# Five weight loads into freed work space, a product on another engine, a new head and order, and identity transposes in a drain

## The chip, the cores and the metric

One core of one Trainium2 chip runs the whole program. The metric is the device time in microseconds (us) of one execution. TensorE (PE) multiplies and transposes, VectorE (DVE), ScalarE (ACT) and GpSimd (POOL) do the rest, SyncE (SP) issues the loads and stores. Inputs and outputs lie in HBM; engines work on SBUF, and PE writes PSUM.

## The reference

All values are float32. A pack attention with 8 batches, 8 heads, 576 tokens of 64 channels and 32 packed queries, and then a soft mixture of 8 experts on the 4608 tokens of 512 channels that come out:

```python
def sm_attn(qq, kk, vv):
    s = scale * qq @ kk.transpose(0, 1, 3, 2)
    a = np.exp(s - s.max(-1, keepdims=True))
    return (a / (a.sum(-1, keepdims=True) + 1e-9)) @ vv
p_packed = sm_attn(p, k, v)              # 32 rows for each head
x = sm_attn(q, p_packed, p_packed)       # as [4608, 512]
logits = x @ phi                         # [4608, 32]
slot_input = softmax(logits, axis=0).T @ x           # 32 slots, 4 for each expert
slot_out[e] = relu(slot_input[e] @ w1[e]) @ w2[e]    # w1 512x1024, w2 1024x512
out = softmax(logits, axis=1) @ slot_out
```

## The kernel before

The attention runs in 8 steps `i` (two batches `dd` = i // 2, four heads). A step transposes k on DVE (`kt`), multiplies it with the packed queries (`s1`, line 355), takes maximum and exponential (`mx1`, `e1`), transposes that (`ap`), multiplies with v (`m`, 408), divides (`rz`, `ppa`, `pp`), transposes (`pt`, `ptc`), transposes q (`qp`, `qc`), multiplies (`s2`, 526) and does the second softmax: maximum `mx2`, subtraction `sb`, exponential `e2`, sum `z2` (on POOL, in the last step on DVE), reciprocal `rc`, product `n2` (POOL); `a2p` and `a2c` transpose it. After every second step the logits of one `dd` are made (`lg`, 631) and joined to a running softmax over all tokens: `f1` and `f3` take the maximum on DVE, `f2` and `f4` turn it around on PE, `f5` takes the exponential `dL` and its sum `zg` on ACT, `rw` (line 701, DVE) multiplies the sum into a 128x32 matrix, `f6` (706) sums that over the partitions on PE, `fd` transposes `dL`, `gr` (734), `rt`, `gt` (753), `rb` and `gs` (780) add the slots' inputs, `fl` copies the logits.

The order of all these pieces on each engine is the text `ORDER`: one word for each piece, with its indices, its PSUM bank after @ and the copying engine after a colon. Each engine executes its share in that order and waits where an input isn't there. What comes last I call the drain: from the last `s2` to the line that writes `xz`, the input of the experts.

The loads go through one ring of 120 KB for each partition, in the order p, then k, q, v of each step, then the 16 halves of w1 (1 MB each) and w2 in 17 pieces (15 of 1 MB, two of 0.5 MB). `pump()` issues the next load on SP as soon as its place in the ring has been released in program order. 14 pieces of the weights fit while the attention still holds its work tiles in the pools `wpool` and `dpool`; the 19 others wait until `layer1a` has read the first ones. After the drain, `layer1a` (868) and `layer1b` make the hidden values, `layer2` (920) runs for experts 0 to 6, `cq` and `cp` prepare the softmax over the slots for the output (`cT`), four tiles at a time, and `last2` (997), line 1010 and line 1018 end the last expert. Then 36 products write the output (1042, 1049), and SP stores it (1044, 1055).

```python
def f_rw(dd, j, bank, eng):
    nc.vector.tensor_scalar_mul(rw, rep[:, 0], zg)
...
for n, e in enumerate(range(1, E - 1)):
    cq(4 * n + 8)
    layer2(e)
    cp(4 * n + 8, "av"[n % 2])
cq(32)
cp(32, "a")
```

Of the kernel before, what the change touches and what calls it, by code (L numbers as in the profile page):

```python
# [15 lines left out]

ORDER = """
p.0.0 p.1.0 px.0.0@7 p.2.0 p.3.0 px.1.0@6 pc.0.0:v kt.0.0  # L20
kt.0.1 px.2.0@7 pc.1.0:v kt.0.2 px.3.0@6 pc.2.0:v kt.0.3 pc.3.0:v
s1.0.0@0 qp.0.0@7 mx1.0.0 qp.0.1@6 qc.0.0:a qp.0.3@5 qc.0.1:a qp.0.4@7
e1.0.1 qc.0.3:v qp.0.2@6 qp.0.5@4 e1.0.0 qc.0.4:v qc.0.2:a ap.0.0@7
rz.0.0 qc.0.5:a ap.0.1@6 apc.0.0:a ap.0.2@5 apc.0.1:a m.0.0@6 apc.0.2:a
kt.1.1 m.0.1 kt.1.0 m.0.2 kt.1.2 ppa.0.1 ppa.0.0 pp.0.1
pp.0.0 kt.1.3 pt.0.0 ptc.0.1:a s1.1.0@0 ptc.0.0:a mp.0.0 mx1.1.0
mm.0.0:a s2.0.0@5 e1.1.1 s2.0.1 e1.1.0 qp.1.1@4 mx2.0.0 ap.1.0@3
qc.1.1:a ap.1.1@2 apc.1.0:a ap.1.2@4 sb.0.0 apc.1.1:a qp.1.0@3 apc.1.2:a
# [1060 lines left out]
```

## Time and profile before

| what | us |
|---|---|
| median of 3 runs (lowest, highest) | 238.25 (237.82, 238.55) |
| the profiled execution's own time | 237.79 |
| its span, first to last instruction | 236.0 |
| busy PE / DVE / ACT / POOL | 182.5 / 126.1 / 92.8 / 47.4 |

The busy times are shares of the whole span. The kernel has stages with different limits, so the rows further down are read by stage. A row of the timeline gives the start and the length of a group of instructions of one line, and in brackets how long the engine had been idle before it and for whom. [...]

### The profile page before, as it was taken

What the parts mean: (1) busy time and instruction counts of PE and PEld (TensorE: products, weight loads), DVE (VectorE), ACT (ScalarE), POOL (GpSimd) and SP (SyncE); (2) the same over time, 40 slices, a digit from 0 to 9 for tenths busy, and PEclk for the clock granted to TensorE, in tenths of its full rate; (3) what the DMA queues carried; (4) which work ended last, traced back from release to release, by engine and by line L of the source; (5) the groups of instructions that cost most, each with busy time, mean ns of one, the idle gap of its engine ahead of it and who ended that gap; (6) DMA issues with size and microseconds to landing.
All of it is one profiled execution on the core that took longest, in us unless ns stands there. A gap on an engine that the chain in (4) does not pass through costs nothing.

```text
span 236.0 us, 6352 instructions
## 1 busy us (share of the span) xinstructions
PE 182.5 (77%) x2715; PEld 117.0 (50%) x2715; DVE 126.1 (53%) x248; ACT 92.8 (39%) x228; POOL 47.4 (20%) x76
## 2 busy tenths in 40 slices
PE   0987989999799995999997577899959655989000
PEld 0665858777496773486866533423311111457000
DVE  1785769676872886464757942772133022159200
ACT  0073847657568574347673422011100000059300
POOL 8100071535305344005458200000000000000000
PEclk9999999999999997799999675579995996599755
DMA  7999999999999999922919000099999998019997
GB/s 161 383 392 391 390 391 390 390 387 391 391 392 388 405 406 403 406 90 60 417 62 350 13 0 0 3 330 431 422 418 422 422 422 332 6 59 409 416 416 301
DMA packets 24683, 72.29 MB, mean 306 GB/s; under 512 B 4176, under 2 KB 4432, under 8 KB 22736
## 3 DMA queue, kind: packets, MB, share of 16 engines
q1 hardware_dynamic: 24080, 71.83, 79.0%
q8 instruction: 21, 0.34, 0.6%
q10 hardware_dynamic: 576, 0.07, 0.2%
q14 instruction: 6, 0.05, 0.1%
HBM read 62.46 MB, written 9.44 MB: 305 GB/s over the span
## 4 chain that ended last, share of the span: by engine, by line
PE 46%; DMA 17%; DVE 17%; ACT 8%; issue 2%; POOL 1%; POOLq 1%; ACTq 0%; DVEq 0%; SPq 0%
DMA ring<-in_moe_w_dram 15%; PE ps L355 6%; PE ps L408 5%; PE ps L868 4%; PE ps L498 4%; PE ps L526 4%; PE ps L1049 3%; PE ps L734 3%; PE ps L607 3%; DVE rw L701 3%; PE ps L386 3%; DVE kT L341 2%; ACT a L369 2%; DMA ring<-in_p_dram 2%; DVE a L557 2%
## 5 line engine op out<-in xcount | busy, mean ns | idle before, releaser
L920 PE MATMUL ps<-ring,hT 128*32 128x512 f32 x112 | 17.7, 722 | 9.4 <-DMA ring<-in_moe_w_dram 9.4
L583 POOL TENSOR_TENSOR zt<-a 128x576 f32<-128x576 f32 x7 | 9.9, 1408 | 72.2 <-ACT a L575 72.2
L341 DVE STREAM_TRANSPOSE kT<-ring 128x576 f32<-128x576 f32 x32 | 23.2, 754 | 1.0 <-DMA ring<-in_k_dram 1.0
L498 PE MATMUL ps<-ident,ring 128*128 128x128 f32 x144 | 20.4, 279 | 0.0
L526 PE MATMUL ps<-ppT,qT 128*64 128x64 f32 x576 | 18.5, 223 | 0.3 <-ACT mm L291 0.3
L598 POOL TENSOR_TENSOR a<-a,zs 128x1152 f32<-128x1152 f32 (+1 forms) x8 | 16.2, 2020 | 12.3 <-DVE zs L594 10.6
L291 ACT COPY qT<-ps 128x512 f32<-128x512 f32 (+1 forms) x43 | 17.9, 477 | 1.7 <-PE ps L498 1.3
L408 PE MATMUL ps<-ring,a1T 64*64 64x128 f32 x576 | 18.2, 272 | 0.3 <-ACT a1T L291 0.3
L291 ACT CAST cT<-ps 128x512 fp32r<-128x512 f32 x6 | 3.5, 586 | 37.1 <-PE ps L946 37.1
L526 PEld LDWEIGHTS ps<-ppT,qT 128*64 128x64 f32 x576 | 17.5, 138 | 0.7 <-ACT mm L291 0.4
L408 PEld LDWEIGHTS ps<-ring,a1T 64*64 64x64 f32 x576 | 15.8, 133 | 2.7 <-DVE rz L421 0.8
L868 PE MATMUL ps<-ring,xz 128*32 128x512 f32 x128 | 16.7, 678 | 0.4 <-DVE xz L953 0.4
L498 PEld LDWEIGHTS ps<-ident,ring 128*128 128x128 f32 x144 | 15.7, 141 | 2.5 <-issue 1.3
L355 PE MATMUL ps<-kT,pT 32*32 32x288 f32 x512 | 16.4, 446 | 0.7 <-issue 0.4
L366 DVE TENSOR_REDUCE nm<-ps 128x2 f32<-128x1152 f32 x8 | 10.9, 1356 | 10.3 <-PE ps L355 8.7
L549 DVE TENSOR_REDUCE mx<-ps 128x36 f32<-128x1152 f32 (+1 forms) x9 | 12.8, 1421 | 4.5 <-PE ps L526 3.4
L369 ACT ACTIVATE a<-ps,nm 128x576 f32<-128x576 f32 x16 | 11.8, 743 | 6.7 <-DVE nm L366 6.7
L607 PE MATMUL ps<-ident,a 128*128 128x128 f32 x72 | 11.9, 303 | 2.8 <-POOL a L598 1.4
L295 DVE CAST cT<-ps 128x512 fp32r<-128x512 f32 x3 | 2.1, 692 | 21.3 <-PE ps L946 21.3
L291 ACT COPY a1T<-ps 128x384 f32<-128x384 f32 x24 | 10.1, 487 | 6.3 <-PE ps L386 6.3
L291 ACT COPY a2T<-ps 128x384 f32<-128x384 f32 x23 | 10.0, 484 | 4.0 <-PE ps L607 4.0
L586 POOL TENSOR_TENSOR zt<-zt 128x288 f32<-128x288 f32 (+2 forms) x21 | 11.2, 535 | 1.6
(130 smaller groups left out, 286.1 us busy)
## 6 DMA issues: line engine op xcount, KB each, us to landing
ring<-in_moe_w_dram SPq DMA_DIRECT2D x31, 1024.0 KB, 13.7
ring<-in_k_dram SPq DMA_DIRECT2D x16, 576.0 KB, 11.9
ring<-in_q_dram SPq DMA_DIRECT2D x16, 576.0 KB, 11.9
ring<-in_v_dram SPq DMA_DIRECT2D x16, 576.0 KB, 12.0
out_dram<-ring SPq DMA_DIRECT2D x10, 768.0 KB, 8.3
ring<-in_moe_w_dram SPq DMA_DIRECT2D x2, 512.0 KB, 18.0
out_dram<-ring SPq DMA_DIRECT2D x2, 512.0 KB, 3.8
ring<-in_p_dram SPq DMA_DIRECT2D x1, 512.0 KB, 4.3
```

The lines of the kernel that those rows point to most:

```text
L291: nc.scalar.copy(dst, src)
L341: nc.vector.transpose(kT[:, b2, :, c].rearrange("p m (t r) -> p m t r", t=T), view(f"k{i}.{b2}").rearrange("p (m t c d) -> p m t c d", m=2 ...
L355: nc.tensor.matmul(ps[32 * y : 32 * y + 32, z, 0 : 32 * T], pT[rs, dd, m, b2, g, c], kT[rs, b2, m, c], start=(c == 0), stop=(c == 1),)
L369: nc.scalar.activation(a1[:, :, x].rearrange("p t (h r) -> p h t r", h=2), s1v[:, x].rearrange("p h (t r) -> p h t r", t=T), AF.Exp, bias= ...
L408: nc.tensor.matmul(ps[64 * b2 : 64 * b2 + 64, b + x, 0:P].rearrange("p (m d) -> p m d", m=2), a1T[rs, t, b2], view(f"v{i}.{b2}").rearrange ...
L498: nc.tensor.transpose(ps[:, bank, o : o + P], view(f"q{i}.{b2}")[:, P * y : P * y + P], ident)
L526: nc.tensor.matmul(psf[64 * b2 : 64 * b2 + 64, o : o + 2 * NS].rearrange("p (u s) -> p u s", u=2), qT[:, b2, n, 64 * x : 64 * x + 64], col ...
L549: nc.vector.tensor_reduce(part(mxs[i % 2], c), s2v(i, c), axis=AX.X, op=ALU.max)
L598: (nc.vector if eng == "v" else nc.gpsimd).tensor_tensor(a, a, z.unsqueeze(3).broadcast_to([P, a.shape[1], a.shape[2], NS]), op=ALU.mult)
L607: nc.tensor.transpose(ps[:, bank, o : o + P], a2s[i // NG % 2][:, t, i % NG].rearrange("p c s -> p (c s)"), ident,)
L868: nc.tensor.matmul(ps[32 * a : 32 * a + 32, b + nh, :], xzf[:, (4 * e + a) * NSLOT : (4 * e + a + 1) * NSLOT], wv[:, j, nh * 512 : (nh + 1 ...
L920: nc.tensor.matmul(ps[32 * a : 32 * a + 32, SO, :], hTf[:, (NJ * e + j) * NSLOT : (NJ * e + j + 1) * NSLOT], w2v(e, j), start=(e == 0 and ...
```

## The change

Five parts. (1) At the point `late`, where `wpool` is given up, five tiles `ext` of 8 KB for each partition are laid into its space, and the next five pieces of the weights are loaded there. Two tiles that the drain still writes or reads change pools for it: `a2_0` and `ppT` go to `wpool`, so that their space is freed too, and the clearing of `hT` and the copy `identr` move behind the drain. `cT` lies in the space of `ext` afterwards, so all `cp` now come after `layer2(1)`, two for each expert. (2) `rw` is made on ACT, inside `f5`. (3) `p` is loaded in four pieces, three of them behind the first k; the first exponential, on a dummy, comes before ACT issues the loads of `phi`; `sel` is built earlier. (4) A new `ORDER`; `s2` is made, and its maximum and subtraction taken, in two halves that may lie in different banks; `gt` is split into two halves by columns. (5) `w.n` puts n transposes of the identity on PE, into a bank that nobody reads, 75 in all, from the last `gr` but one to the experts' first product.

```diff
@@ ORDER: two lines of the last third @@
-fd.3.0 rw.3.0 gr.3.0@4 f6.3.0 rt.3.1:a rt.3.0:a gz.3.0 gt.3.0
+w.6.0@6 f1.3.0 f2.3.0 w.14.0@6 f3.3.0 f4.3.0 w.12.0@6 f5.3.0
...
@@ loads @@
-    loads.append(("p", B * NG * D, p.rearrange("b (g h) s d -> (h s) (b g) d", g=NG)))
+    loads.append(("p0", 2 * NG * D, rows_p(0)))
     for i in range(NSTEP):
         for b2 in range(2):
             loads.append((f"k{i}.{b2}", 2 * T * D, rows9(k, i, b2)))
+        if i == 0:
+            for dd in range(1, ND):
+                loads.append((f"p{dd}", 2 * NG * D, rows_p(dd)))
...
@@ head @@
+    nc.vector.memset(ones, 1.0)
+    first = const.tile([P, 1], F32, name="first")
+    nc.scalar.activation(first, ones[:, 0:1], AF.Exp)
...
-    a2s = [dpool.tile([P, T, NG, 4, NS], F32, name=f"a2_{x}") for x in range(2)]
+    a2s = [wpool.tile([P, T, NG, 4, NS], F32, name="a2_0"), a2_1]
...
-    ppTs = [dpool.tile([P, 2, 2, 4, NS], F32, name=f"ppT_{x}") for x in range(2)]
+    ppTs = [wpool.tile([P, 2, 2, 4, NS], F32, name=f"ppT_{x}") for x in range(2)]
...
@@ f_f5 (and f_rw is gone) @@
+        nc.scalar.mul(rw, rep[:, 0], zg)
         if dd > 0:
             nc.scalar.activation(al, ps[:, b, W2 : W2 + NSLOT], AF.Exp)
-    def f_rw(dd, j, bank, eng):
-        nc.vector.tensor_scalar_mul(rw, rep[:, 0], zg)
...
@@ new @@
+    def f_w(n, j, bank, eng):
+        for _ in range(n):
+            nc.tensor.transpose(ps[:, bank, 0:P], ident, ident)
...
@@ f_late @@
-        hT = late.tile([P, E, NJ * NSLOT + SPE], F32, name="hT")
-        nc.gpsimd.memset(hT, 0.0)
...
+        ext = [extp.tile([P, 2 * FF], F32, name=f"ext_{x}") for x in range(NEXT)]
+        if "at" in state:
+            state["off"] = state.pop("at")[1]
+        for x in range(NEXT):
+            key, width, src = loads[state["next"]]
+            where[key] = (ext[x], width)
+            load(ext[x][:, 0:width], src)
+            state["next"] += 1
...
@@ experts @@
-    cp(0, "a")
-    cq(4)
     layer1b(0)
...
-    for n, e in enumerate(range(1, E - 1)):
-        cq(4 * n + 8)
+    layer2(1)
+    ees.close()
...
+    cp(0, "a")
+    for e in range(2, E - 1):
+        for n in range(2):
+            t0 = 8 * (e - 2) + 4 * n
+            if t0 + 4 < NT:
+                cq(t0 + 4)
         layer2(e)
-        cp(4 * n + 8, "av"[n % 2])
-    cq(32)
-    cp(32, "a")
+        for n in range(2):
+            t0 = 8 * (e - 2) + 4 * n
+            if t0 + 4 < NT:
+                cp(t0 + 4, "av"[n])
```

SP's queue from the last v load to the first store, before (`ring` is the load ring, `x16` a count of like loads):

```order
L167 DMA ring<-in_v_dram 128x2x576 x2
L167 DMA ring<-in_moe_w_dram 128x2x1024 x16
L167 DMA ring<-in_moe_w_dram 128x2048 x15
L167 DMA ring<-in_moe_w_dram 128x1024 x2
L1044 DMA out_dram<-ring 128x256 x2
```

And now:

```order
L158 DMA ring<-in_v_dram 128x2x576 x2
L158 DMA ring<-in_moe_w_dram 128x2x1024 x14
L158 DMA ext_1891<-in_moe_w_dram 128x2x1024
L158 DMA ext_1892<-in_moe_w_dram 128x2x1024
L158 DMA ext_1893<-in_moe_w_dram 128x2048
L158 DMA ext_1894<-in_moe_w_dram 128x2048
L158 DMA ext_1895<-in_moe_w_dram 128x2048
L158 DMA ring<-in_moe_w_dram 128x2048 x12
L158 DMA ring<-in_moe_w_dram 128x1024 x2
```

The two last halves of w1 and the three first pieces of w2 go to `ext`; 14 pieces (13 MB) are left for the ring behind them, where there were 19 (18 MB).

PE in the drain, before, from the last `lg` to the first product of the experts (643 is `f2`, 665 and 673 `f4`, 734 `gr`, 706 `f6`, 753 `gt`, 780 `gs`):

```order
L631 MATMUL ps<-a2T_144,mm_154 32x288 x4
L643 MATMUL ps<-ident,nml 1x128
L665 MATMUL ps<-ones,m_175 128x1
L673 MATMUL ps<-dm,ones 128x32
L734 MATMUL ps<-a_1_142,d 32x256 x18
L706 MATMUL ps<-rw,ones 128x32
L753 MATMUL ps<-rep,rt 128x32 x4
L780 MATMUL ps<-rb,pp_148 64x64 x2
L780 MATMUL ps<-rb,pp_149 64x64 x2
L868 MATMUL ps<-ring,xz 32x512 x48
```

And now, from behind the last `lg` to before `gs` (662 is `f2`, 684 and 692 `f4`, 723 `f6`, 751 `gr`, 771 `gt`, 782 the identity transposes):

```order
L782 MATMUL ps<-ident 128x128 x6
L662 MATMUL ps<-ident,nml 1x128
L782 MATMUL ps<-ident 128x128 x14
L684 MATMUL ps<-ones,m_185 128x1
L692 MATMUL ps<-dm,ones 128x32
L782 MATMUL ps<-ident 128x128 x12
L723 MATMUL ps<-rw,ones 128x32
L782 MATMUL ps<-ident 128x128 x2
L751 MATMUL ps<-a_1_108,d 32x256 x18
L782 MATMUL ps<-ident 128x128 x6
L771 MATMUL ps<-rep,rt 64x32 x8
L782 MATMUL ps<-ident 128x128 x6
```

Between any two products of the chain stands a group of transposes, `f6` comes ahead of `gr`, and `gt` has eight products of half the columns.

SP's head, before, with what each load waits for (DMAHW0 to 3 are the four `phi` loads, 4 to 7 the first loads of SP, and so on around):

```order
L167 DMA ring<-in_p_dram 128x16x64
L167 DMA ring<-in_k_dram 128x2x576 x2
L167 DMA ring<-in_q_dram 128x2x576
L167 DMA ring<-in_q_dram 128x2x576 [waits DMAHW0_49]
L167 DMA ring<-in_v_dram 128x2x576 [waits DMAHW1_49]
L167 DMA ring<-in_v_dram 128x2x576 [waits DMAHW2_49]
```

And now:

```order
L158 DMA ring<-in_p_dram 128x4x64
L158 DMA ring<-in_k_dram 128x2x576 x2
L158 DMA ring<-in_p_dram 128x4x64
L158 DMA ring<-in_p_dram 128x4x64 [waits DMAHW0_49]
L158 DMA ring<-in_p_dram 128x4x64 [waits DMAHW1_49]
L158 DMA ring<-in_q_dram 128x2x576 [waits DMAHW2_49]
L158 DMA ring<-in_q_dram 128x2x576 [waits DMAHW3_49]
```

Both loads of q now stand behind a wait for a `phi` load, where the first of them stood ahead of these waits.

## Rows read from the trace of the kernel before

**Rows 1.** The span by stretches; columns: stretch, length, busy times, PEclk, DMA share, GB/s.

```profile
23.30:87.00 63.70, 60.01 (x1273) 46.80 (x1272) 46.52 (x81) 40.46 (x102) 22.73 (x25) 1.00 1.05 392
87.00:99.00 12.00, 8.77 (x134) 5.18 (x132) 7.83 (x16) 4.87 (x17) 4.24 (x6) 0.72 1.02 407
99.00:125.80 26.80, 26.22 (x521) 21.32 (x523) 14.86 (x32) 17.74 (x47) 9.84 (x12) 1.00 0.47 174
125.80:150.80 25.00, 17.07 (x187) 11.67 (x183) 15.06 (x36) 5.97 (x16) 5.09 (x5) 0.69 0.17 67
150.80:174.50 23.70, 22.46 (x188) 7.38 (x188) 11.59 (x24) 4.00 (x6) 0.00 (x0) 0.89 0.89 355
174.50:196.70 22.20, 14.00 (x88) 3.29 (x88) 4.26 (x14) 1.17 (x2) 0.00 (x0) 0.85 1.01 421
196.70:210.30 13.60, 10.84 (x59) 4.92 (x60) 3.29 (x8) 2.07 (x5) 0.00 (x0) 0.62 0.21 84
210.30:236.00 25.70, 8.47 (x35) 5.88 (x34) 9.49 (x16) 9.89 (x20) 0.00 (x0) 0.70 0.91 367
```

**Rows 2.** The chain of waits in the experts' stage: start, length, what.

```profile
176.86 19.83 DMA ring<-in_moe_w_dram
```

**Rows 3.** The timeline of the head: start, length, engine, line, operation, count, idle before.

```profile
0.73 2.67 ACTq L234 DMA_DIRECT2D phi_sb<-in_moe_phi_dram  x4
...
3.22 1.69 SPq L167 DMA_DIRECT2D ring<-in_q_dram  x2
...
13.27 2.26 PE L498 MATMUL ps<-ident,ring 128*128 128x128 f32 x18
...
19.61 0.78 DVE L341 STREAM_TRANSPOSE kT<-ring 128x576 f32<-128x576 f32 x1 [0.72 <-DMA ring<-in_k_dram]
...
21.72 1.60 PE L355 MATMUL ps<-kT,pT 32*32 32x288 f32 x64
```

**Rows 4.** The waits of SP's queue: total, times, longest.

```profile
SPq L167 <- DMA phi_sb<-in_moe_phi_dram: 3.4, 3, 1.5
```

**Rows 5.** The tile of phi: its loads from issue to landing.

```profile
DMA to landing us min/median/max: 3.8/4.9/6.6
```

**Rows 6.** The timeline around the second running softmax.

```profile
90.20 2.12 POOL L598 TENSOR_TENSOR a<-a,zs 128x1152 f32<-128x1152 f32 x1 [0.77 <-DVE zs L594]
90.32 2.04 DVE L701 TENSOR_SCALAR rw<-rep,zg 128x32 f32<-128x32 f32 x1
...
92.51 0.60 PE L706 MATMUL ps<-rw,ones 128*128 128x32 f32 x2 [2.79 <-DVE z_run L714]
```

**Rows 7.** The timeline of the drain.

```profile
125.96 3.45 DVE L701 TENSOR_SCALAR rw<-rep,zg 128x32 f32<-128x32 f32 x1
...
126.87 1.49 PE L734 MATMUL ps<-a,d 64*32 64x256 f32 x36
...
127.56 1.83 POOL L808 MEMSET hT<- 128x2080 f32 x1
...
131.78 1.26 ACT L575 ACTIVATE a<-a 128x640 f32<-128x640 f32 x2 [2.73 <-DVE z_run L714]
...
135.36 1.54 PE L607 MATMUL ps<-ident,a 128*128 128x128 f32 x6 [1.37 <-POOL a L598]
...
143.67 2.77 PE L734 MATMUL ps<-a,d 64*32 64x256 f32 x36 [1.40 <-DVE d L691]
```

**Rows 8.** The timeline of SP's queue behind the drain.

```profile
152.78 2.64 SPq L167 DMA_DIRECT2D ring<-in_moe_w_dram  x3
...
210.28 0.83 SPq L1044 DMA_DIRECT2D out_dram<-ring  x2
```

**Rows 9.** The timeline of layer 2 and of the last expert on PE.

```profile
174.52 1.07 PE L920 MATMUL ps<-ring,hT 128*32 128x512 f32 x8 [1.23 <-DMA ring<-in_moe_w_dram]
...
196.73 1.86 PE L920 MATMUL ps<-ring,hT 128*32 128x512 f32 x8 [1.43 <-DMA ring<-in_moe_w_dram]
...
205.46 1.86 PE L997 MATMUL ps<-ring,hT 128*32 128x256 f32 x16
```

More of the change, by code (lines that the diff above doesn't have):

```diff
@@ new lines @@
+mp.2.0 m.3.2 mx2.2.2 mm.2.0:a lg.0.0@5 sb.2.2 ppa.3.1 ppa.3.0
+pp.3.1 e2.2.0 pp.3.0 qp.3.4@4 f1.0.0 qp.3.0@3 qc.3.4:v f2.0.0
+z2.2.0:p qp.3.1@2 qc.3.0:a f3.0.0 qp.3.3@4 qc.3.1:a qp.3.2@3 qp.3.5@1
+pt.3.0 qc.3.3:v qc.3.2:a f4.0.0 qc.3.5:a ptc.3.0:a s1.4.0@0 ptc.3.1:v
+f5.0.0 fd.0.0 f6.0.0 mx1.4.0 mp.3.0 mm.3.0:a s2.3.0@6 rc.2.0
+e1.4.1 gz.0.0 n2.2.0:p s2.3.1@2 e1.4.0 mx2.3.1 sb.3.1 gr.0.0@0
+mx2.3.2 sb.3.2 kt.5.2 e2.3.0 kt.5.1 a2p.2.2@7 a2p.2.0@6 rt.0.0:a
+rt.0.1:v z2.3.0:p a2c.2.2:a a2p.2.1@4 kt.5.0 gt.0.0 a2c.2.0:a a2c.2.1:a
@@ new lines @@
+lg.2.0@7 ppa.7.1 z2.6.0:p ppa.7.0 pp.7.1 qp.7.3@6 pp.7.0 f1.2.0
+qp.7.0@3 qc.7.3:a f2.2.0 qp.7.4@2 qc.7.0:v qp.7.1@6 qc.7.4:a f3.2.0
+qp.7.5@3 qp.7.2@1 pt.7.0 qc.7.1:a qc.7.5:a qc.7.2:a ptc.7.1:v ptc.7.0:a
+f4.2.0 rc.6.0 mp.7.0 f5.2.0 s2.7.0@2 n2.6.0:p mm.7.0:v fd.2.0
+f6.2.0 s2.7.1@4 mx2.7.1 gz.2.0 a2p.6.2@6 mx2.7.2 a2p.6.1@1 a2c.6.2:a
+a2p.6.0@0 sb.7.1 a2c.6.1:a a2c.6.0:a gr.2.0@2 late.0.0 sb.7.2 fl.2.0
+e2.7.3 e2.7.4 w.10.0@7 z2.7.3:v rt.2.1:a rt.2.0:a rc.7.3 gt.2.0
+z2.7.4:v n2.7.3:p w.8.0@6 rc.7.4 rb.2.0 n2.7.4:v gs.2.0 a2p.7.0@7
@@ L144, in view, with load @@
     def view(key):
-        off, width = where[key]
-        return ring[:, off : off + width]
+        place, width = where[key]
+        return ring[:, place : place + width] if isinstance(place, int) else place[:, 0:width]
+    def load(dst, src):
+        shape = src.shape[1:]
+        if len(shape) == 2:
+            dst = dst.rearrange("p (a b) -> p a b", a=shape[0])
+        elif len(shape) == 3:
+            dst = dst.rearrange("p (a b c) -> p a b c", a=shape[0], b=shape[1])
+        nc.sync.dma_start(out=dst, in_=src)
     def free(off, width):
@@ L160, in pump @@
             where[key] = (off, width)
-            dst = ring[:, off : off + width]
-            shape = src.shape[1:]
-            if len(shape) == 2:
-                dst = dst.rearrange("p (a b) -> p a b", a=shape[0])
-            elif len(shape) == 3:
-                dst = dst.rearrange("p (a b c) -> p a b c", a=shape[0], b=shape[1])
-            nc.sync.dma_start(out=dst, in_=src)
+            load(ring[:, off : off + width], src)
             state["next"] += 1
@@ L751, in f_gt @@
         for a in range(4):
-            o = 2 * P + a * NSLOT
-            nc.tensor.matmul(
-                ps[:, b, o : o + NSLOT],
-                rt[:, a].rearrange("p b w s -> p (b w s)"),
-                rep[:, 0],
-                start=True,
-                stop=True,
-            )
+            for b2 in range(2):
+                o = 2 * P + a * NSLOT
+                nc.tensor.matmul(
+                    ps[64 * b2 : 64 * b2 + 64, b, o : o + NSLOT],
+                    rt[:, a, b2].rearrange("p w s -> p (w s)"),
+                    rep[:, 0],
+                    start=True,
+                    stop=True,
+                )
+    def f_w(n, j, bank, eng):
+        for _ in range(n):
+            nc.tensor.transpose(ps[:, bank, 0:P], ident, ident)
     def f_rb(dd, j, bank, eng):
@@ L827, in pack_attention_soft_moe @@
         fs[n](int(i), int(j), int(bank) if bank else None, eng)
[L830 removed]
+    xz, xzf = lt["xz"], lt["xzf"]
     Lf = L_sb.rearrange("p a t s -> p (a t) s")
```

186 lines of the change are left out of this document (88 added, 98 removed).

## The prediction

> **What bounds the kernel now.** I read the span by stretches first, then the chain of waits, then the timeline where these two point. The stretches [rows 1] show four stages with different limits. From 23.3 to 125.8 PE is busy for 95.0 of 102.5 us: the attention is bound by PE, although the loads run at 390 GB/s beside it, for they run ahead. One stretch in it is poor: 87 to 99, with PE busy for 8.77 of 12 us and a mean clock of 0.72. From 125.8 to 150.8 comes the drain, a chain through PE, DVE, ACT and POOL: PE is busy for 17.07 of 25.0 us, the clock is 0.69, and the DMA moves 67 GB/s, since the ring is full of weights that nobody can read yet. From 150.8 to 196.7 the experts wait for weights at 355 and 421 GB/s; one piece of the chain alone is 19.83 us of their loads [rows 2]. From 196.7 to 210.3 a serial end runs at a clock of 0.62, and then the output leaves at 367 GB/s for 25.7 us.
>
> So loads are what the experts lack, and in the drain the DMA has nothing to do. The change moves five of 19 late pieces from the one to the other.
>
> **The experts' stage.** In layer 2, groups of eight matmul instructions wait for one piece each; the first starts at 174.52, the last of ten at 196.73 [rows 9], so a piece takes 22.21 / 9 = 2.47 us. SP issues the first late piece at 152.78 [rows 8], 2.0 us after the stage begins. The piece of 196.73 is the 16th: 43.95 us after the first issue, of which 16 x 2.47 = 39.5 are transfer and 4.4 lead. The last two MB follow at 196.73 + 4.9 = 201.7, the first store at 210.28 [rows 8]. From the stage's begin to the store: 59.5 us.
>
> Now 14 pieces are late, and the piece for the end of expert 6 is the 11th. The first issue waits for eight instructions of layer 1; these ran at the lower clock and, by the drain's transposes (below), will run at the upper: 1.1 us for 2.0. So the 11th is there at 1.1 + 4.4 + 27.2 = 32.7 us, the last at 37.6.
>
> PE must keep up. It was busy for 22.46 us at 0.89 in the stretch to 174.5 [rows 1], 20.0 us of work at the upper clock; that holds both layers 1, experts 0 and 1, and three groups of transposes for the output (0.5 us each, by 18 transposes in 2.26 us [rows 3]), of which one is left there: 19.0. Then four experts at 2 x 1.07 us [rows 9] with two such groups each, and one without: 14.7. Expert 6 ends at 33.7, against 32.7 + 1.07 = 33.8 by the DMA. They are level; I add 0.5 us for handing over.
>
> Behind the last landing 8.6 us passed before the store, since `cp` for the last tiles, the first half of the last expert and line 1010 all came after expert 6. Now no `cp` stands there, and the first half needs only a piece that lands 2.5 us earlier. What must follow the last landing is the last half piece and its end: from 205.46 to 210.28 [rows 8, 9], less half of the 1.86 us of that group, 3.9 us. Begin to store: 37.6 + 3.9 + 0.5 = 42.0 instead of 59.5, **-17.5 us**. Of it 12.3 are the five pieces, 0.9 the earlier first issue, 4.7 the tail, less 0.5. The `ext` loads must be done before this counts. They stand in SP's queue behind the ring's 14; the first two wait for ACT only, the third for the last `s2`, the fourth for the last `gr` but one and POOL. From the drain's begin they need 4.4 + 12.3 = 16.7 us, and the drain keeps 21 (below). The clearing of `hT` (1.83 us on POOL [rows 7]) now falls beside layer 1; `hT` is first read after 10 us of it, so I cost it at nothing, and at 1.8 us if DVE were held by it all the way.
>
> **The drain.** At 125.96 `rw`, a product of 32 columns, takes 3.45 us on DVE while POOL clears `xz` and `hT`; at 90.32 the same line takes 2.04 beside a POOL product of 2.12 [rows 6, 7]. `mx2`, `sb` and `gz` queue behind it, and the last exponential comes at 131.78 having waited 2.73 for `gz` [rows 7]. With `rw` on ACT, behind `dL` and ahead of `f6`, I credit 2.4 of the 3.45, because the second half of `s2` and `gz` still have to come first. POOL's other clear, `xz`, stays there.
>
> PE's 17.07 busy us at 0.69 are 11.8 at the upper clock: -5.3. The price is 75 transposes at 2.26 / 18 = 0.126 us, 9.4 us, in waits that were 25.0 - 17.07 = 7.9 long and of which the 2.4 are gone: 5.5 remain, so the transposes overrun the waits by 3.9. The longest, 14 in one group (1.76 us), stand where PE waited for three short DVE steps. Sum: -2.4 - 5.3 + 3.9 = -3.8, I take **-4**. Bounds: -8, if all 75 are hidden; +11.4, if the clock stays low (a rival below). `gt` in two halves of columns has twice the instructions at half the width; no row shows it, between 0 and +0.5 us each I take 0.
>
> **The attention.** In the stretch 87 to 99 PE waits 2.79 us in one piece for DVE [rows 6], 3.2 in all, and 8.77 us at 0.72 are 2.5 more than at 1.00 [rows 1]: up to 5.7 us, which hang on the same `rw`. Other waits of PE from 23.3 to 125.8 come to 3.7 + 0.6 = 4.3 us. A new order may lose some and make others; `mx2` and `sb` in halves let ACT and POOL start earlier, at some added DVE time. I take **-4**, with bounds of -10 (all waits and the low clock gone) and +3 (the old stall gone, and as many new waits as the old order had, twice over).
>
> **The head.** A smaller first `p` brings the first product forward, but it doesn't count for long: step 1 waits for its k. DVE waited at 19.61 for its landing, and `s1` ran at 21.72 [rows 3]. These loads come later now. SP's fifth load waits for the first of the `phi` loads, and so on for four; before, SP lost 3.4 us in three such waits [rows 4], with `phi` issued from 0.73 on [rows 3]. Now ACT's table load and dummy come first, `phi` needs 3.8 to 6.6 us to land [rows 5], and both q loads, which SP issued from 3.22 on [rows 3], wait for the third and fourth of them. Even without the table load the third lands at 0.73 + 1.3 + 3.8 = 5.8 at the earliest, 2.6 us behind 3.22. The DMA runs on meanwhile with what was issued, so I estimate the loads 2 us later at step 1, and PE 0.5 us later, since it had slack there: **+0.5**, between -1 and +3.
>
> **Sum.** 237.79 - 17.5 - 4 - 4 + 0.5 = 212.8 for an execution like the profiled one, which was 0.46 below the median of its three runs. I forecast **213 us**, with a range of its own from 208 to 218. The 1.8 us around the span and the 25.7 of the output stay.
>
> **Rivals.**
> - *The transposes don't hold the clock.* For it: at 135.36 six transposes of the drain took 1.54 us, 0.257 each, and the last `gr` 2.77 against 1.49 at 126.87 [rows 7]. Against: the attention, where transposes and small products follow each other without gaps, has a clock of 1.00 [rows 1]; no row holds transposes alone. Then 75 x 0.257 = 19.3 us stand in 5.5 of waits, +13.8, less the 2.4, +11.4 in the drain; the experts begin at the lower clock and give back 15.5. 237.8 + 11.4 - 15.5 - 4 + 0.5 = 230 us. [...] Chance 0.12.
> - *PE bounds layer 2 at the lower clock.* A group takes 1.86 us there instead of 1.07 [rows 9], a `cp` 1.0 for 0.5: 4 x 5.7 + 3.7 = 26.5 for 14.7, so 225 us. For it: the group at 196.73 ran so, after a wait of 1.43. Against: the loads lead PE until expert 6, and it waits for nothing before. Chance 0.08.
> - *The `ext` loads come late.* If a release holds SP until the drain ends, the 12.3 us return: 225 us. Chance 0.04.
> - *More is gained.* The attention loses all its waits (-10), the rest as forecast: 207 us. Chance 0.12.
> - *Slower.* The new order makes PE wait in every step, for example for the halved DVE work ahead of `s2`'s successors. The rest gains 21 us over eight steps, so it decides from 2.6 us more a step; the longest single wait on DVE was 2.79 and came once [rows 6]. At 3.5 us a step: 245 us. Chance 0.03.
>
> **Chances.** The forecast keeps 0.61. The range of 205 to 225 us takes in the cases at 207 and 225 and leaves out 230, 245 and the tails of the forecast's bounds, near 0.2. A change under 0.3% cannot be told from none here; no case lies there, the gap between 225 and 245 holds it with 0.01. Slower 0.03, faster 0.96.
>
> **What would show it.** Five loads to `ext` that land before the experts' first product; layer 2 groups with waits only at experts 5 and 6; a first store some 42 us after that product; no DVE row of `rw` and no wait of over 2 us ahead of `f6`; a clock near 1.00 through the drain. Wrong would be: single transposes of 0.2 us or more there, groups of layer 2 at 1.86, a begin of the experts' stage later than 146, or k of step 1 landing after 23.

## The result and the profile after

The changed kernel takes **216.38 us** (median of 4 executions, 215.27 to 218.44) against 238.03 for the one before on the same chip; the ratio is 0.910, with an interval of 0.903 to 0.918. The forecast was 213 (205 to 225). The profiled execution took 215.27 us, with a span of 213.5. Some executions of one kernel are longer than its others at a lower granted clock (in after_again below 252.38 us at 0.66 beside 213.86 at 0.97): the medians are of all executions, the ratios leave the long ones out.

The stretches of the kernel after; the columns are those of [rows 1]: stretch, length, busy times of PE, PEld, DVE, ACT and POOL, PEclk, DMA share, GB/s. PEclk is the mean granted clock of PE. In the traces of before and after the clock is either 1.00 or 0.50 at any time (in before 1.00 from 130 to 132 us, 0.50 from 133 to 136); "upper" and "lower" stand for these two.

```profile
23.30:87.00 63.70, 57.30 (x1203) 45.87 (x1205) 51.84 (x102) 35.74 (x92) 21.50 (x24) 0.97 1.05 387
87.00:99.00 12.00, 11.60 (x301) 9.52 (x302) 9.94 (x20) 5.29 (x15) 3.71 (x6) 1.00 0.78 296
99.00:125.80 26.80, 22.42 (x448) 18.61 (x449) 19.46 (x43) 14.90 (x38) 12.16 (x13) 1.00 0.70 266
125.80:150.80 25.00, 23.64 (x306) 16.47 (x306) 15.98 (x38) 6.70 (x16) 4.58 (x5) 1.00 0.71 277
150.80:174.50 23.70, 23.56 (x224) 9.16 (x220) 12.71 (x35) 3.52 (x6) 0.00 (x0) 1.00 1.01 423
174.50:196.70 22.20, 17.67 (x113) 9.82 (x105) 13.08 (x27) 10.93 (x24) 0.00 (x0) 1.00 0.71 284
```

Two things went as planned. The stretch from 87 to 99 is full (11.60 of 12 us, clock 1.00, against 8.77 at 0.72), and the drain has a clock of 1.00 and moves 277 GB/s, where it had 0.69 and 67. But from 23.3 to 87 and from 99 to 125.8 PE is busy for 2.7 and 3.8 us less than before: waits that were not there.

SP's queue after the last v load, in the timeline of the kernel after (start, length, line, what):

```profile
122.55 7.96 SPq L158 DMA_DIRECT2D ext<-in_moe_w_dram  x5
147.55 18.91 SPq L158 DMA_DIRECT2D ring<-in_moe_w_dram  x14
187.59 0.83 SPq L1080 DMA_DIRECT2D out_dram<-ring  x2
```

The five `ext` loads are issued in the drain; the ring's 14 follow 1.08 us after the experts' first product (146.47), and the first store comes 41.1 us after it, where it took 59.5 [rows 8]. The experts wait for weights in only two places of PE's timeline, for the 11th and 12th late piece:

```profile
179.01 1.07 PE L942 MATMUL ps<-ring,hT 128*32 128x512 f32 x8 [1.40 <-DMA ring<-in_moe_w_dram]
181.49 1.07 PE L1033 MATMUL ps<-ring,hT 128*32 128x256 f32 x16 [1.41 <-DMA ring<-in_moe_w_dram]
```

PE in the drain (L543 is the last `s2` half, L782 the identity transposes, L751 `gr`, L890 layer 1):

```profile
125.34 1.27 PE L543 MATMUL ps<-ppT,qT 128*64 128x64 f32 x36
...
137.36 1.69 PE L782 MATMUL ps<-ident 128*128 128x128 f32 x14
138.98 0.38 PE L684 MATMUL ps<-ones,m 1*128 1x1 f32 x2
...
139.54 1.53 PE L782 MATMUL ps<-ident 128*128 128x128 f32 x12
...
141.52 1.49 PE L751 MATMUL ps<-a,d 64*32 64x256 f32 x36
...
146.47 1.94 PE L890 MATMUL ps<-ring,xz 128*32 128x512 f32 x16
```

A transpose takes 0.12 us (1.69 / 14) and the last `gr` 1.49, where it took 2.77 [rows 7]. The drain takes 19.9 us for 23.9.

And the new waits. Two of them are the largest of PE in the attention, and what ended them is "issue": nothing that the profile shows (L370 is `s1`, L423 `m`, L543 `s2`).

```profile
42.35 1.60 PE L370 MATMUL ps<-kT,pT 32*32 32x288 f32 x64
43.89 0.87 PE L423 MATMUL ps<-ring,a1T 64*64 64x128 f32 x21
46.72 0.43 PE L423 MATMUL ps<-ring,a1T 64*64 64x128 f32 x3 [1.96 <-issue]
...
94.75 1.67 PE L370 MATMUL ps<-kT,pT 32*32 32x288 f32 x64
96.35 2.25 PE L543 MATMUL ps<-ppT,qT 128*64 128x64 f32 x69
101.04 0.33 PE L543 MATMUL ps<-ppT,qT 128*64 128x64 f32 x3 [2.44 <-issue]
```

Both stand three products before the end of a group whose other products had the same inputs. I call such an idle time without a releaser a stand.

The stages of each profiled execution, in us, from the starts and lengths of the same rows: to the end of the last `s2`; the drain, to the experts' first product; from there to the first store; the output.

| kernel | to last s2 | drain | experts | output | median us |
|---|---|---|---|---|---|
| before | 126.9 | 23.9 | 59.5 | 25.7 | 238.0 |
| after | 126.6 | 19.9 | 41.1 | 25.9 | 216.4 |
| after_again | 128.2 | 19.9 | 42.4 | 25.9 | 217.9 |
| no_w | 129.0 | 21.2 | 42.2 | 25.9 | 219.0 |
| w_trim | 127.3 | 18.2 | 42.5 | 25.9 | 215.1 |
| old_order | 125.7 | 19.9 | 40.9 | 25.7 | 214.0 |
| no_ext | 127.8 | 19.9 | 55.0 | 25.9 | 228.9 |
| rw_dve | 134.8 | 19.8 | 42.6 | 25.8 | 219.7 |
| before_rw_act | 122.5 | 22.1 | 59.8 | 25.7 | 231.5 |
| ext_act | 122.8 | 22.7 | 42.0 | 25.6 | 215.7 |
| shift32 | 128.2 | 19.9 | 40.9 | 25.8 | 217.8 |
| best | 122.6 | 20.9 | 43.6 | 25.7 | 213.9 |

A row is one trace. The changed kernel's drain comes out the same in all six traces that have it whole (19.8 to 19.9), so small differences there can be read. The other two columns can't be read so finely: the same attention ends between 126.6 and 129.0 in after, after_again, no_w, w_trim and no_ext, and the experts' stage of the same kernel is 41.1 in after and 42.4 in after_again. The last weights land 37.5 and 37.2 us after the stage's begin in these two; the difference lies behind that, where the last stretch has a clock of 1.00 in after and 0.92 in after_again:

```profile
174.50:196.70 22.20, 18.57 (x117) 10.24 (x115) 11.13 (x24) 8.62 (x19) 0.00 (x0) 0.92 0.64 258
```

### The profile page after: what moved, and what is told of

Same layout as the page of the kernel before. It is cut to its first block, busy times and chain, and to the rows that moved or that the text cites. A ratio compares the mean times of both kernels' runs of the same rounds, so it can differ in the third digit from the quotient of the medians.

```text
span 213.5 us, 6572 instructions
## 1 busy us (share of the span) xinstructions
PE 173.1 (81%) x2822; PEld 120.1 (56%) x2822; DVE 136.6 (64%) x286; ACT 85.4 (40%) x206; POOL 47.3 (22%) x75
## 4 chain that ended last, share of the span: by engine, by line
PE 41%; DMA 22%; DVE 14%; ACT 9%; issue 5%; SPq 1%; ACTq 0%; DVEq 0%
DMA ring<-in_moe_w_dram 15%; PE ps L543 7%; PE ps L423 5%; DMA ring<-in_k_dram 5%; PE ps L370 5%; PE ps L513 5%; PE ps L401 4%; ACT ring L321 3%; PE ps L782 3%; DVE a L576 3%; DMA phi_sb<-in_moe_phi_dram 3%; PE ps L626 3%; DVE mx L568 2%; ACT a L384 2%; PE ps L890 2%
## 5 line engine op out<-in xcount | busy, mean ns | idle before, releaser
L543 PE MATMUL ps<-ppT,qT 128*64 128x64 f32 x576 | 20.0, 224 | 4.4 <-issue 2.4
L543 PEld LDWEIGHTS ps<-ppT,qT 128*64 128x64 f32 x576 | 18.2, 138 | 6.2 <-issue 4.3
L423 PE MATMUL ps<-ring,a1T 64*64 64x128 f32 x576 | 18.9, 273 | 2.0 <-issue 2.0
L423 PEld LDWEIGHTS ps<-ring,a1T 64*64 64x64 f32 x576 | 15.8, 133 | 5.3 <-issue 4.1
L370 PE MATMUL ps<-kT,pT 32*32 32x288 f32 x512 | 16.3, 446 | 2.9 <-DVE kT L356 2.7
L568 DVE TENSOR_REDUCE mx<-ps 128x18 f32<-128x576 f32 x16 | 11.9, 746 | 7.7 <-PE ps L543 7.7
L321 ACT COPY qT<-ps 128x512 f32<-128x512 f32 (+1 forms) x32 | 14.1, 486 | 5.1 <-PE ps L513 4.9
L890 PE MATMUL ps<-ring,xz 128*32 128x512 f32 x112 | 12.5, 593 | 0.0
L370 PEld LDWEIGHTS ps<-kT,pT 32*32 32x32 f32 x512 | 7.3, 107 | 8.8 <-DVE kT L356 3.8
L576 DVE TENSOR_TENSOR a<-ps,mx 128x576 f32<-128x576 f32 x16 | 11.9, 754 | 0.3
L594 ACT ACTIVATE a<-a 128x1152 f32<-128x1152 f32 (+2 forms) x9 | 9.5, 1061 | 6.6 <-DVE a L576 6.5
L942 PE MATMUL ps<-ring,hT 128*32 128x512 f32 x88 | 10.9, 599 | 1.4 <-DMA ring<-in_moe_w_dram 1.4
L401 PE MATMUL ps<-ident,a 128*128 128x128 f32 x72 | 10.7, 294 | 1.3 <-ACT a2T L321 0.7
L605 POOL TENSOR_TENSOR zt<-zt 128x288 f32<-128x288 f32 (+2 forms) x21 | 11.2, 531 | 1.6
L321 ACT COPY a2T<-ps 128x384 f32<-128x384 f32 x20 | 8.7, 483 | 6.4 <-PE ps L626 6.4
## 6 DMA issues: line engine op xcount, KB each, us to landing
ext<-in_moe_w_dram SPq DMA_DIRECT2D x5, 1024.0 KB, 11.2
```

The source lines that it names most:

```text
L321: nc.scalar.copy(dst, src)
L370: nc.tensor.matmul(ps[32 * y : 32 * y + 32, z, 0 : 32 * T], pT[rs, dd, m, b2, g, c], kT[rs, b2, m, c], start=(c == 0), stop=(c == 1),)
L401: nc.tensor.transpose(ps[:, bank, o : o + P], a1[:, t].rearrange("p x r -> p (x r)"), ident)
L423: nc.tensor.matmul(ps[64 * b2 : 64 * b2 + 64, b + x, 0:P].rearrange("p (m d) -> p m d", m=2), a1T[rs, t, b2], view(f"v{i}.{b2}").rearrange ...
L543: nc.tensor.matmul(psf[64 * b2 : 64 * b2 + 64, o : o + 2 * NS].rearrange("p (u s) -> p u s", u=2), qT[:, b2, n, 64 * x : 64 * x + 64], col ...
L568: nc.vector.tensor_reduce(part(mxs[i % 2], c), s2v(i, c), axis=AX.X, op=ALU.max)
```

## The experiments

**after_again**: the changed kernel once more, as the base of the next three.

> The changed kernel once more. In its profile PE stands still twice in the attention with no releaser shown, 1.96 us in the middle of the products with v (line 423, at 44.8) and 2.44 us in the middle of a second score product (line 543, at 98.6), and its four runs spread over 3.2 us where those of the kernel before spread over 1.1. Theory A: the two stalls belong to a place in PE's instruction stream, so they stand again at the same two instructions with about the same lengths, and the time is 215 to 217. Theory B: they come by chance, from blocks of PE's instructions that arrive late between the loads; then they stand elsewhere or are missing, and the time moves by up to 4.4 us with them (211 to 218).

217.94 us, ratio 0.9065 (0.899 to 0.915). Both stands are at the same instructions again, three before the end of the groups of L423 and L543, with 1.96 and 3.01 us. So they belong to a place in PE's program, not to a chance of the run. The length of the second does change: 2.44 us in after, 3.01 here, 0.61 in no_ext. So theory A holds for the place and not for the length.

**no_w**: without the identity transposes.

```diff
...
-w.6.0@6 f1.3.0 f2.3.0 w.14.0@6 f3.3.0 f4.3.0 w.12.0@6 f5.3.0
+f1.3.0 f2.3.0 f3.3.0 f4.3.0 f5.3.0
...
```

> The changed kernel without the 75 identity transposes. Theory: they hold PE at the upper clock. Without them the granted clock falls in the drain; its PE work grows by some 5 us and the overrun of 3.9 us goes, so the time from the last second score product to the experts' first product stays near 20 us (19.5 to 22), and the experts begin at the lower clock (their first 64 instructions in 9.6 us as before, not 6.9). Time 217 to 220. [...]

219.01 us, ratio 0.925 (0.920 to 0.930). The drain's stretch and the last `gr` of no_w:

```profile
125.80:150.80 25.00, 17.07 (x247) 11.47 (x251) 15.24 (x39) 6.67 (x21) 6.44 (x5) 0.75 0.73 290
```

```profile
143.68 2.77 PE L751 MATMUL ps<-a,d 64*32 64x256 f32 x36
```

The clock falls to 0.75 and `gr` takes 2.77 us again. So it is the transposes that hold the clock at 1.00 in this drain, and nothing else in it does. In the stages they give 1.3 us in the drain and 1.0 behind it, of which 0.9 is the first reload (1.95 us after the stage's begin for 1.08). The time agrees: it is 2.6 us above the changed kernel's 216.38, and its interval lies clear of both of that kernel's (0.903 to 0.918, and 0.899 to 0.915 in after_again). The theory was right.

**w_trim**: 49 transposes for 75, the fewer where they overran.

```diff
...
-w.6.0@6 f1.3.0 f2.3.0 w.14.0@6 f3.3.0 f4.3.0 w.12.0@6 f5.3.0
+w.4.0@6 f1.3.0 f2.3.0 w.4.0@6 f3.3.0 f4.3.0 w.9.0@6 f5.3.0
...
```

> The changed kernel with 49 identity transposes instead of 75: each group cut to about the length of the wait that it stands in (14 to 6, 12 to 9, 7 to 3, the groups of 6 to 4 or 3, 2 to 1). Theory: the overrun of the long groups is on the drain's chain and the rest still holds the clock at 1.00: the drain is 1.5 to 2.5 us shorter, 214 to 215. Rival: with fewer of them the clock falls somewhere in the drain, and it is as long as or up to 3 us longer than with 75, 216 to 219.

215.06 us, ratio 0.907 (0.901 to 0.912). (The group of 14 became 4, where the expectation says 6.) The drain is 1.7 us shorter, 18.2 us, and its clock stays at 1.00: 26 of the transposes cost more than they gave. The experts take 1.4 us longer, all of it behind the last landing, where the clock of their last stretch is 0.92. after_again has the same long end with all 75 transposes, so nothing shows that the trim caused it. The time can't be told from the changed kernel's.

**old_order**: the changed kernel with the head and the order of the attention of before, `rw` on ACT; drain and experts as changed.

```diff
-p.0.0 px.0.0@7 kt.0.0 pc.0.0:a kt.0.1 kt.0.2 kt.0.3 p.1.0
+(the ORDER of before up to the last s2, without rw)
...
-    loads.append(("p0", 2 * NG * D, rows_p(0)))
+    loads.append(("p", B * NG * D, p.rearrange("b (g h) s d -> (h s) (b g) d", g=NG)))
...
```

> The changed kernel with the head (one load of p, phi ahead of the dummy exponential) and the attention order of the kernel before, up to the last step's second score product; the product on ScalarE, the loads into freed space, the drain and the experts as changed. Theory: the forecast of 4 us for the attention failed because the new order makes as many new waits on PE as the one it takes away (its PE is idle for 11.2 us from 23.3 to 126.6, where 7.5 us and 2.5 us of low clock stood before); the old order without its wait for DVE then ends the attention 3 to 5 us earlier than either, at 121.5 to 123.5, time 211 to 213.5. Rival: the old order only moves its wait, because POOL's product and clears hold DVE at the next instruction, and the attention ends at 126 to 127 again, time 215 to 217.

213.99 us, ratio 0.904 (0.899 to 0.909). The last `s2` ends at 125.7, 0.9 earlier than in after and not at 121.5 to 123.5: neither theory nor rival met it. The new head and order gain nothing: that is the forecast's attention term gone. Beside before_rw_act (below), which has the same order nearly up to there, it is 3.2 us late. 2.0 of that are longer waits of the kind that shift32 explains (3.7 for 1.7 us in all), 0.6 a later start, and 0.7 the last `s2` itself, whose halves keep the new place with `f6` between them (122.72 to 125.71, where before_rw_act has 120.17 to 122.49). One of the longer stands (1.20 us idle at 113.3) has no counterpart in before_rw_act: `gt` stays in halves here, 16 PE instructions more for each `dd`, so the blocks that shift32 explains end 32 instructions earlier in the program by then. Why two others are 0.3 to 0.4 us longer stays open.

**no_ext**: without the five early loads.

```diff
-NEXT = 5
+NEXT = 0
```

> The changed kernel without its five early loads: the space of ext stays empty and all 19 late pieces come through the ring again, as before; everything else as changed. My theory: five pieces of 2.47 us are late again, so the stretch from the experts' first product to the first store goes from 41 to 53 us, and the whole time rises by 12 us, to 226 to 229 us. Rival A: the loads were hidden anyway and the gain of the experts' stage came from the shorter tail and the clock; then the time rises by less than 4 us. Rival B: the five loads slow the drain's or the attention's own work down, so that the drain without them is more than 1 us shorter than 19.9 us (last s2 to the experts' first product); I expect it the same within 0.5.

228.94 us, ratio 0.968 (0.957 to 0.979). The experts' stage is 13.9 us longer and the drain the same to 0.1, so the loads cost the drain nothing. The last piece lands 49.8 us after the stage's begin for 37.5, and these 12.3 us are the five pieces; the other 1.6 are the longer end that after_again has too. Layer 2 waits for every piece again, as before the change (start to start of two groups, 2.5 us a piece):

```profile
172.41 1.07 PE L942 MATMUL ps<-ring,hT 128*32 128x512 f32 x8 [1.42 <-DMA ring<-in_moe_w_dram]
175.07 1.07 PE L942 MATMUL ps<-ring,hT 128*32 128x512 f32 x8 [0.78 <-DMA ring<-in_moe_w_dram]
177.56 1.07 PE L942 MATMUL ps<-ring,hT 128*32 128x512 f32 x8 [1.42 <-DMA ring<-in_moe_w_dram]
```

**rw_dve**: the changed kernel with `rw` back on DVE.

```diff
-        nc.scalar.mul(rw, rep[:, 0], zg)
+        nc.vector.tensor_scalar_mul(rw, rep[:, 0], zg)
```

> The changed kernel with rw, the product of 32 columns, back on DVE instead of ACT, at the same place in the order. My theory: DVE takes 2 to 3.5 us for it wherever POOL works on a large tile at the same time, as before; one or two of the three such places in the attention and the one in the drain come back, so +2 to +5 us, 218 to 221. Rival: the old stalls hung on the old order, in which rw stood beside POOL's longest products; in the new one it costs its own 0.2 us each, and the time stays within 1 us.

219.68 us, ratio 0.918 (0.903 to 0.933). The time decides nothing: the median lies where the theory had it, and the interval holds the changed kernel's 0.910. The trace is of an execution of 224.84 us, so I read only single rows from it. The four `rw` in DVE's timeline:

```profile
70.71 0.24 DVE L706 TENSOR_SCALAR rw<-rep,zg 128x32 f32<-128x32 f32 x1
...
94.27 0.24 DVE L706 TENSOR_SCALAR rw<-rep,zg 128x32 f32<-128x32 f32 x1 [1.04 <-ACT rt L698]
...
131.25 1.85 DVE L706 TENSOR_SCALAR rw<-rep,zg 128x32 f32<-128x32 f32 x1 [0.46 <-ACT rt L698]
...
148.69 0.24 DVE L706 TENSOR_SCALAR rw<-rep,zg 128x32 f32<-128x32 f32 x1 [1.90 <-ACT rt L698]
```

Only one of the four is long. It holds up `f6` and with it the second half of the last `s2`, which starts 2.72 us after the first half; in after it is 1.51, so this `rw` costs 1.2 us. The drain behind it takes 19.8 us, as with `rw` on ACT. So in the new order `rw` seldom meets a product of POOL, and the trace is nearer to the rival.

**before_rw_act**: the kernel before, with `rw` on ACT and nothing else.

```diff
@@ f_f5 (and every rw in ORDER is gone) @@
+        nc.scalar.mul(rw, rep[:, 0], zg)
-    def f_rw(dd, j, bank, eng):
-        nc.vector.tensor_scalar_mul(rw, rep[:, 0], zg)
```

> The kernel before with one edit: rw on ACT behind dL instead of on DVE; the order is otherwise the old one. My theory: the stall of 2.79 us in the stretch 87 to 99 goes (it has 1.00 as its clock then), and the drain loses 2.4 us: 232 to 235 us. Rival: the waits only change their name, since the second half of s2, gz and POOL's products come last there anyway: 236.5 to 238.5 us.

231.48 us, ratio 0.977 (0.966 to 0.989): -6.2 us (1.1 to 3.4%), by one line. The stretch from 87 to 99, and the last `s2` and the experts' first product:

```profile
87.00:99.00 12.00, 10.99 (x198) 8.07 (x198) 9.61 (x21) 8.44 (x25) 3.88 (x5) 1.00 1.02 406
```

```profile
120.17 2.32 PE L526 MATMUL ps<-ppT,qT 128*64 128x64 f32 x72
...
144.60 13.11 PE L866 MATMUL ps<-ring,xz 128*32 128x512 f32 x96 [0.45 <-DVE xz L951]
```

The last `s2` ends at 122.5, 4.4 us earlier than before and 4.1 earlier than in the changed kernel. ext_act and best, with the same order, end it at 122.8 and 122.6. So the order of before had all of the attention's gain within it, and the changed kernel doesn't have it.

**before_ext**: the kernel before with the five early loads and what they need.

```diff
+NEXT = 5
...
@@ ORDER: late.0.0 stands behind gr.2.0@6 now, and not ahead of mx2.7.1 @@
...
@@ f_late: ext and its loads, as in the change @@
+        ext = [extp.tile([P, 2 * FF], F32, name=f"ext_{x}") for x in range(NEXT)]
@@ experts: hT, identr and cp behind the drain, as in the change @@
```

> The kernel before with one part: the five loads into the freed work space with what they need (the two tiles in the other pool, hT's clearing and the copy of the identity behind the drain, and the softmax for the output behind the second expert); order, head, rw and a drain without identity transposes as before. My theory: the five pieces' 12.3 us and part of the tail's 4.7 come off: 222 to 226 us, with the drain's 23.9 us shorter by at most 1. Rival: PE at the lower clock of a drain without transposes can't keep up in the experts' layer 1 and 2, and gives back half: 228 to 232 us.

220.49 us, ratio 0.932 (0.921 to 0.942), three of four executions within 219.9 to 220.9; the profiled one was disturbed (842.58 us), so no trace of it is used. -17.2 us against the 237.73 of the kernel before in the same round: more than either theory gave. The time alone shows nothing that a drain without transposes took back. The edit also moves POOL's two clears behind the `rw` that took 3.45 us beside them, so a part of the 17.2 may be that; without a trace it stays open.

**ext_act**: the two diffs above together, on the order of before.

> The kernel before with two parts of the change: the five early loads (with what they need) and rw on ACT. Head, order of the attention and the drain without transposes as before. If the two parts add up as they stood alone (-17.3 and -6.3 us against 237.7), 214 us: as fast as or faster than the whole change, which then got nothing from its new order, head and transposes together. Rival: the new order and head are worth something beside them; then this is above 217 us.

215.70 us, ratio 0.909 (0.905 to 0.914): as fast as the whole change, and 1.5 us short of the two parts' sum. Against the changed kernel it has 3.9 us less to the last `s2`, and 2.9 and 0.9 more in the drain and the experts' stage. What the new drain and its transposes gained, the attention of the changed kernel lost.

**shift32**: what the stands are. The trace of the changed kernel has 22 transfers of 16 KB on the queue named "instruction", 0.36 MB in the page's list of queues, and one of them lies at each stand:

```profile
q8 instruction: 22, 0.36, 0.7%
```

PE has 5644 instructions there, weight loads and products; 5644 / 256 is 22.05. I counted PE's records: the stands of every kernel lie 256 apart or a multiple of it, up to a few records (2037 between the two of after, for 8 x 256 = 2048). The kernel before has one too, in the middle of `s1`:

```profile
34.63 0.71 PE L355 MATMUL ps<-kT,pT 32*32 32x288 f32 x14 [0.44 <-issue]
```

The next rows are worked out from the records of single transfers, in us from the block's first instruction. "Ran" goes to the start of the block's last instruction, so a stand measured from start to start is longer than the idle time in the timeline (0.84 for 0.44 us in the last row):

```
kernel, block from  ran   transfer  landed  ran on  landed to on
after       40.52   3.97      3.85    4.96    6.19          1.24
after       94.88   3.50      3.80    4.76    6.16          1.39
w_trim      40.88   3.97      3.76    4.85    6.20          1.35
old_order  107.25   4.58      3.76    4.68    6.05          1.36
before      28.52   5.27      3.67    4.72    6.11          1.39
```

In these rows the next block begins to come some 3.8 us after PE enters one, while the loads fill the DMA, and lets PE go on after 6.05 to 6.2 us. A block that needs more than that hides it. The figure isn't fixed. The block from 94.88 in after is the same 256 instructions in four more traces, and the next one's transfer begins 2.0 us after its entry in no_ext (DMA at 251 GB/s until then), 3.2 in no_w and w_trim (311 and 315), 3.8 in after (315) and 4.3 in after_again (379); PE goes on after 4.35, 5.6, 5.6, 6.2 and 6.7 us. To test what the stands are I put 64 instructions ahead of everything, which PE runs while it has nothing to do:

```diff
+    def f_u(n, j, bank, eng):
+        for _ in range(n):
+            nc.tensor.transpose(ps[0:32, bank, 0:32], ident[0:32, 0:32], ident[0:32, 0:32])
...
-p.0.0 px.0.0@7 kt.0.0
+u.32.0@3 p.0.0 px.0.0@7 kt.0.0
```

> The changed kernel with 32 small transposes (32x32 of the identity, read by nobody) as PE's first work, while PE waits for p; they are 64 more instructions of PE, a weight load and a product each. Nothing behind them is changed. Theory: PE gets its instructions in blocks of 256, the block behind is asked for when PE enters one, and while the loads run it is there only 6.1 us later; so a block that PE could run in less makes it stand for the rest at the block's end. From the trace of the changed kernel, in which blocks of 3.97 and 3.50 us ended in stands of 2.2 and 2.7 us, I move the ends 64 instructions ahead. Then the stand of 1.96 us inside L423 and that of 2.44 us inside L543 (three before the end of either group) are gone; new ones are 1.8 us between a group of L543 and one of L626 at about 37.4 us, 1.4 us in the middle of the group of 72 of L543 at about 97.5 us (36 before it, 36 behind), and about 1 us each near 67.5 and 80.2 us. The sum is 6.9 us for 5.8, so the time is 0 to 2 us above that of the changed kernel. Rival: the stands belong to the products themselves or to what they wait for; then they stay at the same three last products of L423 and L543, with 1.96 and 2.4 us.

217.82 us, ratio 0.921 (0.914 to 0.928). PE's timeline at the place foretold, and at that of the old second stand:

```profile
37.87 1.25 PE L543 MATMUL ps<-ppT,qT 128*64 128x64 f32 x36
41.52 1.65 PE L626 MATMUL ps<-ident,a 128*128 128x128 f32 x9 [2.40 <-issue]
...
99.56 2.32 PE L543 MATMUL ps<-ppT,qT 128*64 128x64 f32 x72
102.01 1.09 PE L513 MATMUL ps<-ident,ring 128*128 128x128 f32 x8
```

Both old stands are gone, and one of 2.40 us (1.8 expected) has come up between L543 and L626, where nothing waited. Of the smaller ones, that near 80.2 came (1.00 us idle, at 82.87), that near 67.5 can't be told from a wait for ACT of 0.97 us at 68.76, and the 1.4 us in the middle of L543 did not come; why is not traced. The time is 1.4 us above the changed kernel's 216.38, within the 0 to 2 foretold. So the stands of this kernel are waits for instructions, at the ends of blocks of 256: the one of 2.40 us, which came where only the count of instructions had changed (by 64), shows it.

**best**: ext_act with 44 transposes in the drain of before.

```diff
...
-a2c.7.2:a lg.3.0@7 f1.3.0 fl.3.0 f2.3.0 f3.3.0 f4.3.0 f5.3.0
+w.3.0@1 a2c.7.2:a lg.3.0@7 w.4.0@1 f1.3.0 fl.3.0 f2.3.0 w.6.0@1 f3.3.0 f4.3.0 w.9.0@1 f5.3.0
...
```

> The kernel before with the five early loads, rw on ACT, and 44 identity transposes in PE's waits of the drain; the order of the attention, the undivided second half steps and the head stay as before. Theory: the last s2 ends at 122.5 us, as in the kernel before with rw on ACT alone (none of PE's blocks of 256 instructions in its attention is shorter than 5.1 us, so the stands for instructions stay under 0.9 us), the drain takes 20 to 21 us at a clock of 1.00, the first store comes 41 us after the experts' first product, and the rest is 25.9 us: 209.5 to 212 us, 4 to 6 below the changed kernel. Rival: the attention of this order takes as long as the changed one as soon as the early loads stand beside it; then 214 to 216 us.

213.86 us, ratio 0.898 (0.893 to 0.904): the lowest of all with old_order (213.99), some 1% below the changed kernel, though the two intervals just touch. The last `s2` ends at 122.6 and the drain takes 20.9, as expected, but the time is above the 209.5 to 212 foretold, since the experts take 43.6 and not 41:

```profile
125.80:150.80 25.00, 21.64 (x207) 12.76 (x208) 16.54 (x35) 6.52 (x16) 3.33 (x3) 0.93 0.68 271
...
174.50:196.70 22.20, 17.26 (x94) 9.63 (x93) 12.15 (x21) 10.98 (x25) 0.00 (x0) 0.92 0.62 249
```

The clock is 0.93 around their begin and 0.92 at their end, where after had 1.00 in both. The begin costs 0.9 us (the first reload comes 1.95 us into the stage for 1.08). The other 1.6 lie behind the last landing, as in after_again, so they are no mark of this kernel.

## Why the prediction was right, and where not

*The sum.* 212.8 was forecast for the profiled execution, and it took 215.27. The attention with the head is 3.2 us above its terms, the experts 0.8 below theirs, and the drain is on its term. So the total is near because the two large terms were right; only 0.8 us of the miss was cancelled.

*The experts' stage, -17.5: right.* 41.1 us for the 42.0 foretold (42.4 in after_again). The first reload came 1.08 us after the stage's begin (1.1), the 11th piece 32.5 after it (32.7). In no_ext the last piece lands 12.3 us later, the forecast for the five pieces. From the last landing to the store are 3.7 us in after (3.9) and 5.3 in after_again, where 8.6 stood before. In ext_act, without transposes, the first reload comes after 1.94 us: the 0.9 was right.

*The drain, -4: right, and by its own terms.* 23.9 to 19.9. `rw` alone gives 1.8 (before_rw_act; 2.4 forecast), the transposes 1.3 (no_w; 5.3 - 3.9 = 1.4 forecast), and what is left, 0.8, goes to the new order, which the forecast didn't count: that the sum fits to 0.1 us is in part luck. That the transposes overrun their waits is shown by w_trim, which wins back 1.7 us with 26 fewer. The credit for `rw` holds on the order of before only: with the new order the drain is as short with `rw` on DVE (rw_dve, 19.8).

*The attention, -4: wrong.* Measured -0.3, head included. The step that failed is not the stall that goes: with `rw` on ACT the stretch from 87 to 99 filled up, and on the order of before that alone gave 4.4 us. What failed is "A new order may lose some and make others", which the sum set at nothing. The changed kernel's attention took 4.1 back. From 23.3 us to the end of the last `s2` PE is idle for 11.2 us there and for 4.9 in before_rw_act. Stands for instructions are 4.4 of the one and 0.9 of the other; waits for DVE and ACT are most of the rest, 6.7 and 3.7. On the other side PE was busy for 1.9 us more up to 23.3. So the stands are the larger part of the new idle time, but not all of it. The two long ones come from density: the new order puts `s1` close to `m` and `s2`, and two blocks of 256 instructions run in 3.97 and 3.50 us. In the order of before none is under 5.16 us, and its stands are 0.8 us at most from start to start. The trace of before had them (0.84 us at 33.8), too small to be noticed, and what they are could have been read there: a block that ran in 5.27 us went on after 6.11. How much of the 4.1 us is the order by itself stays open: old_order, which keeps the halves of `gt` and of the last `s2`, wins back only 0.9.

*The head, +0.5: too high, by little.* The second step's `s1` ends at 22.76 instead of 23.32. q is issued at 6.11 instead of 3.22, as foretold, but it is k that the step waits for, and that landed only 0.9 and 0.2 us later (at 18.31 and 19.77), not 2. The gain is in DVE's order: it now makes the four `kt` of the step in one go and ends at 21.23, where the fourth stood behind `pp` and ended at 21.98.

*The rivals.* "The transposes don't hold the clock" fell: the clock from 125.8 to 150.8 is 1.00 with them (after) and 0.75 without (no_w), and a transpose takes 0.12 us, not 0.257. "PE bounds layer 2 at the lower clock" fell with it: groups take 1.07 us and wait for loads only. `ext` was not late. "More is gained" didn't come. "Slower" needed 2.6 us more in every step; two blocks lost 2.0 and 2.4.

## What to carry to other kernels

Look for a stretch in which the DMA moves little (67 GB/s in the drain here) and for space that is already free in it: five loads brought forward gave 12 to 14 us, more than all work on the order. Before a new order is written for PE where it waits for nothing, count its instructions in blocks of 256 (22 transfers of 16 KB for 5644 instructions here). Beside loads, the next block took 4.35 to 6.7 us to come in these traces, and packing one closer than that won nothing: those that ran in 3.97 and 3.50 us went on after 6.19 and 6.16. Count anew after an edit that changes the number of instructions: with 64 more ahead of everything both long stands were gone and one of 2.40 us stood elsewhere (shift32). Identity transposes held the clock at 1.00 in this drain, where it was 0.75 without them, but one that overruns its wait costs up to its 0.12 us: 26 fewer took 1.7 us off (w_trim).

## What the runs showed of the hardware

The traces show 22 transfers of 16 KB for PE's 5644 instructions in after, and 21 for 5430 in before: one for every 256. While the loads run at 250 to 390 GB/s PE waits for some of them: in the five rows of the table, from entering a block to running on into the next are 6.05 to 6.2 us, of which 3.7 to 3.9 pass before the transfer begins, 0.9 to 1.1 in it and 1.2 to 1.4 behind it. For one block in five traces it is 4.35 to 6.7 us. Where the DMA moves 14 GB/s (106 to 109 us in the kernel after) the transfer begins 0.57 us after the entry. That it is the loads that hold the transfer back fits all of these, but was not tried by itself.

`rw`, the product of 32 columns, took 0.20 to 0.24 us on DVE (before, rw_dve), 1.08 to 3.45 where a long operation of POOL ran beside it, and 0.32 on ACT in all its rows (after, before_rw_act). Each of the four long ones ends 0.02 to 0.04 us after POOL's operation does (62.70 after 62.66, 92.36 after 92.32 and 129.41 after 129.39 in before, 133.10 after 133.06 in rw_dve). Not every DVE line was held so: `mx2` beside the same POOL product took 0.76 us (after, 125.12), as it does behind it (126.66).
